# First batch of an attention-plus-experts kernel: one visit per head with split inputs, two sets of score banks, experts held back

## The chip, the cores and the metric

One core of one Trainium2 chip runs the whole program. The metric is the device time of one execution in microseconds (us), the median of three runs. Five instruction streams work side by side, each in its own fixed order: PE (TensorE, matmuls), DVE (VectorE), ACT (ScalarE), POOL (GpSimd) and SP (SyncE, which here only issues DMA transfers).

## The reference, cut to what matters

```python
batch, n_heads, seq, head_dim = (4, 8, 768, 64)
q_bucket, k_bucket = ...          # 6 sign bits of q @ proj and of k @ proj
mask   = q_bucket[:, :, :, None] == k_bucket[:, :, None, :]
scores = np.where(mask, 0.125 * q @ k.T, -1e9)
attn   = softmax(scores)          # per row; sum + 1e-9 below the line
x      = (attn @ v)  ->  [4 * 768 tokens, 8 * 64]
h      = x @ w_in                 # 512 -> 2048
g      = s * max(h, 0)**2 + b
out    = g @ w_out                # 2048 -> 512
```

All is float32. The first half is called attention below, the second half experts (the kernel's function is `moe`).

## The kernel before, in words

**Slots and visits.** Attention is cut into 96 slots: 4 batches x 8 heads x 3 chunks of 256 queries (`CH`). A visit is a stretch of slots of one head for which the head's inputs lie ready. In a slot, `scores` runs six leading matmuls (keys by queries, with the hash bits as extra rows) into three PSUM banks, DVE takes the maximum over keys (`mx`), PE transposes it, DVE reduces it again (`nmt`), PE transposes that, DVE builds a row of negated maxima (into `bq` or `zhl`), and six more matmuls ("rest") add that row to the banks. ACT takes the exponential of the three banks, and `values` multiplies by v. A reciprocal on DVE, `zpb`, comes once for two heads.

**Precision.** A float32 matmul takes several passes. A split input is a rounded part plus a remainder (`aq`/`bq` for queries, the two planes of `ks` for keys), so that matmuls on rounded operands can be used and the "rest" matmuls carry the remainders. Split inputs are made by `prep`: per head three `split` steps and three `hash_` steps, each PE, ACT and DVE, and then copies between buffers by SP's DMA queue, the last of them only after the third hash.

**The first batch before.** It is visited twice. In visits 0 to 7 (slots 0 to 7) each head's first chunk is computed with unsplit float32 inputs, kept in `EQ` and `EK`, which lie in the buffers that hold weights 16 to 31 later; the leading matmuls of these slots (L523) are full float32. In visits 8 to 15 (slots 8 to 23) the other two chunks of each head follow, from inputs that `resplit` derives from `EQ` and `EK`. Batches 1 to 3 (slots 24 to 95) are visited once, three slots to a visit. In the first batch the products with v are full float32 too (L582); later they use split exponentials, `hl`.

**Weights.** 32 tiles of w_in and w_out are decoded into split form while the first batch runs: a load on ACT's DMA queue, ACT L304 and L305, DVE L306 and L307, POOL L308, ACT L310 and POOL L316 each. `decodes` says how many are begun by slot i.

**Experts.** `moe(bb, c)` is one chunk of 256 tokens, over all eight heads: in 8 groups, 24 matmuls on w_in (L660) into bank 5 and 12 on w_out (L677) into banks 6 and 7. A chunk needs the last head's slot of that chunk number. There are 12 chunks, and `moe` steps have the lowest priority on PE, so they fill what attention leaves. They may start as soon as inputs and weights are there (`GATE = 0`).

**Banks.** Scores use banks 0 to 2 in every slot, so the leading matmuls of one slot wait for the exponentials of the slot before. Bank 3 takes the products with v, bank 4 the small transposes and `prep`.

**Order.** All steps go into `Plan`; `Plan.order` sets every engine's order in advance by a list scheduler with a cost per step, a cost `HOP` for passing a result to another engine, and `LOOK`, how far it will wait for a step of higher priority. On the chip each engine runs that order and waits on semaphores.

Of the kernel before, what the change touches and what calls it, by code (L numbers as in the profile page):

```python
# [22 lines left out]
EPS = 1e-9  # L23
# [8 lines left out]
class Plan:  # L32
# [25 lines left out]
    def order(self):  # L58
# [14 lines left out]
        while len(out) < n:  # L73
# [7 lines left out]
            i = min((i for i in open_[e] if ready[i] <= t + LOOK.get(e, 0.0)), key=lambda i: (self.steps[i][3], i))  # L81
# [22 lines left out]
HOP = {None: 0.0, PE: 0.2, DVE: 0.13, ACT: 0.2, POOL: 0.1, SP: 1.8}  # L104
SAME = {None: 0.0, PE: 0.2, DVE: 0.0, ACT: 0.05, POOL: 0.0, SP: 0.0}
LOOK = {PE: 0.0, DVE: 0.5, ACT: 0.2}
# [3 lines left out]
def lsh_attention_moe(ctx: ExitStack, tc, q, k, v, proj, w_in, w_out, s, b, out):  # L110
# [173 lines left out]
    def decode(u, pr):  # L284
# [19 lines left out]
        act(512, lambda: nc.scalar.activation(g, raw()[:, :, 1].bitcast(F32), AF.Copy, scale=float(2.0**-112)), rk + [("pace", u % PACE)], [gk], pr)  # L304
        act(512, lambda: nc.scalar.activation(raw()[:, :, 0], raw()[:, :, 0].bitcast(U32), AF.Copy, scale=float(2.0**-29)), rk, rk, pr)  # L305
        dve(256, lambda: nc.vector.tensor_scalar(raw()[:, :, 1], gi, -2**31, None, ALU.bitwise_and), [gk], rk, pr, 0.54)  # L306
        dve(512, lambda: nc.vector.scalar_tensor_tensor(gi, gi, 3, raw()[:, :, 1], ALU.logical_shift_left, ALU.bitwise_or), rk, [gk], pr, 0.88)  # L307
# [46 lines left out]
    def prep(w, i, pr):  # L354

        x, y, h, exact = visits[w]["x"], w % 2, visits[w]["h"], w < EARLY
        aq, bq, ks, nat = EQ[h] if exact else AQ[y], BQ[y], KS[y], NAT[y]
# [7 lines left out]
        def both(g, i, pr):  # L365

            pb = fill_bank()
            cols, o = slice(g * HS, (g + 1) * HS), bank[:, pb, 0:HS]

            def tr():  # L370
                for t in range(HT):
                    nc.tensor.transpose(out=bank[:, pb, t * P:(t + 1) * P], in_=nat[:, g * HT + t], identity=ident)
            pe(0.33, tr, NK, [("b", pb)], pr)
            act(HS, lambda: nc.scalar.activation(aq[:, cols], o, AF.Copy, scale=qk_sb), [("b", pb)], AK(x, g=thirds(g)), pr, 0.12)
            dve(HS, lambda: nc.vector.tensor_copy(EK[h][0:D, cols], o[D:P]), [("b", pb)], [("ks", x, g)], pr, 0.5)
            if g:
                ahead(pr)

        def split(g, i, pr):
            cols, o = slice(g * CH, (g + 1) * CH), bank[:, 4, CH:2 * CH]  # L380

            def tr():
                for t in range(TPC):
                    nc.tensor.transpose(out=bank[:, 4, CH + t * P:CH + (t + 1) * P], in_=nat[:, g * TPC + t], identity=ident)  # L384
            pe(0.23, tr, NK, [("b", 4, 1)], pr)
            act(CH, lambda: nc.scalar.activation(aq[:, cols], o, AF.Copy, scale=qk_sb), [("b", 4, 1)], AK(x, g=(g,)), pr, 0.12)
            dve(CH, lambda: nc.vector.scalar_tensor_tensor(bq[:, cols], o, qk_sb, f32(aq[:, cols]), ALU.mult, ALU.subtract), [("b", 4, 1)] + AK(x, g=(g,)), BK(x, g=(g,)), pr, 0.48)
# [408 lines left out]
```

## Time and profile before

| | us |
|---|---|
| median of 3 runs (lowest, highest) | 1117.24 (1116.52, 1120.74) |
| profiled execution, its own time | 1122.19 |
| its span from first to last instruction | 1120.4 |
| PE busy | 1061.0 |
| DVE busy | 657.1 |
| ACT busy | 702.5 |
| POOL busy | 683.9 |

A row of the timeline gives the start, the duration, the engine, the line, the operation, output and inputs, how often, and in brackets the idle time ahead of it and what ended it. A row of windows gives the stretch, its length, for each engine the busy time and in brackets the number of instructions, then the granted clock of PE as a share of full speed, the busy share of the DMA engines and the GB/s moved. A row of groups ends with busy time, mean duration in ns, idle time ahead and what ended that. `x6` in the timeline counts the profile's records; a full float32 matmul leaves two of them.

### The profile page before, as it was taken

How to read it: one execution, taken by the hardware profiler on the slowest of the kernel's cores; microseconds unless marked ns; L12 is line 12 of the kernel's file. 1: busy time of each engine (PE TensorE's matmuls, PEld its weight loads, DVE VectorE, ACT ScalarE, POOL GpSimd, SP SyncE). 2: the span in 40 equal slices, each digit the busy share in tenths (PEclk: the TensorE clock that was granted, in tenths of full speed). 3: DMA queues.
4: the chain of work that ended last, by engine and by line, in shares of the span. 5: the costliest groups of instructions: out<-in, count | busy, mean ns of one | idle time of the engine just before them, and what ended most of it. 6: DMA issues, size and time to landing. Idle time of an engine off the chain costs nothing.

```text
span 1120.4 us, 18819 instructions
## 1 busy us (share of the span) xinstructions
PE 1061.0 (95%) x6862; PEld 919.1 (82%) x6862; DVE 657.1 (59%) x807; ACT 702.5 (63%) x1377; POOL 683.9 (61%) x617
## 2 busy tenths in 40 slices
PE   8998788999999999989999999999999999999998
PEld 6665666878888888778888888888888998898987
DVE  6666576766767776766777676767776752000000
ACT  5556677766677667666767667677776765333332
POOL 5345898876777667656767676767676765222221
PEclk9888899999999999989999999999999999999999
DMA  8644454433322422332333242233233202101010
GB/s 173 160 138 129 131 138 113 131 96 86 89 73 69 133 61 73 90 88 56 78 100 91 53 130 61 76 81 98 63 81 86 70 1 85 39 19 57 1 57 19
DMA packets 99404, 94.49 MB, mean 84 GB/s; under 512 B 68528, under 2 KB 72112, under 8 KB 99312
## 3 DMA queue, kind: packets, MB, share of 16 engines
q1 hardware_dynamic: 94112, 76.24, 26.1%
q10 hardware_dynamic: 5200, 17.05, 5.0%
q8 instruction: 54, 0.88, 0.3%
q14 instruction: 38, 0.31, 0.1%
HBM read 49.81 MB, written 18.87 MB: 61 GB/s over the span
## 4 chain that ended last, share of the span: by engine, by line
PE 80%; DVE 7%; ACT 5%; DMA 3%; POOL 3%; issue 2%; SPq 0%; DVEq 0%; ACTq 0%; POOLq 0%
PE bank L660 23%; PE bank L677 21%; PE bank L555 5%; PE bank L525 5%; PE bank L582 4%; PE bank L585 4%; PE bank L584 4%; PE bank L523 2%; PE bank L534 2%; PE bank L384 2%; PE bank L612 2%; DVE mx L530 2%; DMA xd<-xsb 2%; DMA xc<-xd 1%; ACT et L560 1%
## 5 line engine op out<-in xcount | busy, mean ns | idle before, releaser
L578 POOL TENSOR_TENSOR hl<-et,hl 128x512 fp32r<-128x512 f32 x216 | 278.1, 1317 | 163.0 <-ACT hl L577 147.6
L660 PE MATMUL bank<-xc,w 128*128 128x256 f32 x2304 | 344.8, 288 | 9.5 <-DMA xc<-xd 8.0
L660 PEld LDWEIGHTS bank<-xc,w 128*128 128x128 f32 x2304 | 307.5, 191 | 20.9 <-DMA xc<-xd 9.3
L677 PE MATMUL bank<-w,ghb 128*128 128x512 f32 x768 | 256.3, 397 | 0.0
L668 POOL TENSOR_TENSOR glb<-rb,ghb 128x512 fp32r<-128x512 f32 x96 | 124.4, 1296 | 137.9 <-ACT ghb L667 130.0
L530 DVE TENSOR_REDUCE mx<-bank 128x256 f32<-128x1536 f32 x96 | 168.1, 1752 | 44.0 <-PE bank L525 25.7
L677 PE MATMUL bank<-w,glb 128*128 128x512 f32 x384 | 152.1, 400 | 0.5 <-POOL glb L668 0.5
L665 ACT ACTIVATE rb<-bank 128x512 f32<-128x512 f32 x96 | 57.1, 595 | 151.3 <-PE bank L660 148.7
L677 PEld LDWEIGHTS bank<-w,ghb 128*128 128x128 f32 x768 | 136.7, 189 | 17.2
L560 ACT ACTIVATE et<-bank 128x512 f32<-128x512 f32 x240 | 130.7, 624 | 31.2 <-PE bank L555 27.6
L606 DVE TENSOR_REDUCE zb<-et 128x256 f32<-128x1536 f32 x72 | 126.1, 1751 | 41.3 <-ACT et L560 41.0
L577 ACT CAST hl<-et 128x512 fp32r<-128x512 f32 x216 | 128.6, 661 | 0.8
L584 PE MATMUL bank<-hl,vs 128*128 128x256 f32 x432 | 121.6, 299 | 0.5 <-ACT hl L577 0.5
L525 PE MATMUL bank<-aq,ks 78*128 78x256 f32 x528 | 118.6, 308 | 1.4 <-ACT et L560 0.7
L585 PE MATMUL bank<-hl,vs 128*128 128x256 f32 x432 | 115.8, 288 | 2.9 <-POOL hl L578 2.5
L525 PEld LDWEIGHTS bank<-aq,ks 78*128 78x128 f32 x528 | 91.0, 194 | 12.6 <-ACT ex L560 2.0
L685 DVE SCALAR_TENSOR_TENSOR osb<-bank,misc,bcs 128x512 f32<-128x512 f32 x22 | 16.2, 744 | 132.4 <-PE bank L677 132.4
L585 PEld LDWEIGHTS bank<-hl,vs 128*128 128x128 f32 x432 | 82.5, 191 | 8.8 <-POOL hl L578 6.0
L555 PE MATMUL bank<-bq,ks 128*128 128x256 f32 x528 | 79.5, 287 | 9.6 <-DVE bq L544 8.3
L616 ACT ACTIVATE xpb<-bank,vmn 64x256 f32<-64x256 f32 x96 | 44.9, 468 | 69.3 <-PE bank L585 67.7
L584 PEld LDWEIGHTS bank<-hl,vs 128*128 128x128 f32 x432 | 82.1, 190 | 3.8 <-ACT hl L577 0.7
L622 DVE RECIPROCAL zpb<-zpb 128x256 f32<-128x256 f32 x48 | 83.7, 1743 | 2.3 <-ACT zpb L614 1.9
(111 smaller groups left out, 1662.9 us busy)
## 6 DMA issues: line engine op xcount, KB each, us to landing
xd<-xsb SPq DMA_DIRECT2D x48, 256.0 KB
xc<-xd SPq DMA_DIRECT2D x48, 256.0 KB
raw<-in_moe_w_in_dram ACTq DMA_DIRECT2D x16, 512.0 KB
raw<-in_moe_w_out_dram ACTq DMA_DIRECT2D x16, 512.0 KB
nat<-in_q_dram SPq DMA_DIRECT2D x32, 192.0 KB
nat<-in_k_dram SPq DMA_DIRECT2D x32, 192.0 KB
bq<-aq SPq DMA_DIRECT2D x32, 192.0 KB
out_dram<-osb SPq DMA_DIRECT2D x22, 256.0 KB
```

Source lines behind the costliest of these rows:

```text
L525: nc.tensor.matmul(o, ks[0:HR + TPC, 0, kt], aq[0:HR + TPC, cs], start=m == 0, stop=m == 1, skip_group_check=True)
L530: dve(S * TPC, lambda: nc.vector.tensor_reduce(t, sc, AX.XY, ALU.max), [("b", b) for b in pb], [tk], pr, 1.75)
L555: nc.tensor.matmul(o, ks[:, 1, kt], bq[:, cs], start=False, stop=m == 1, skip_group_check=True)
L560: act(512, lambda p=p, z=z: nc.scalar.activation(et(z) if plain(i) else pairs(z), bank[:, pb[p]] if plain(i) else bank[:, pb[p]].rearrange ...
L577: act(512, lambda z=z, y=y: nc.scalar.copy(HL[2 * y].rearrange("p (m n) -> p m n", n=CH), pairs(z)), [("e", z)], [("hl", 2 * y)], pr)
L578: pool(512, lambda z=z, y=y: nc.gpsimd.tensor_tensor(HL[2 * y + 1].rearrange("p (m n) -> p m n", n=CH), pairs(z), f32(HL[2 * y]).rearrange ...
L584: nc.tensor.matmul(av, VS[w % 2][:, kt], HL[2 * y][:, ms], start=(kt == 0), stop=False)
L585: nc.tensor.matmul(av, VS[w % 2][:, kt], HL[2 * y + 1][:, ms], start=False, stop=(kt == NT - 1))
L606: dve(S * TPC, lambda: nc.vector.tensor_reduce(ZB, es, AX.XY, ALU.add), [("e", z) for z in range(NE)], ["zb"], pr, 1.75)
L660: nc.tensor.matmul(hp, wt[("wi", n, cc)][:, m % 2, fs], xc[:, m // 2, :], start=(cc == 0 and m == 0), stop=(cc == NC_ - 1 and m == 2))
L668: pool(2 * CH, lambda r=r, gh=gh, gl=gl: nc.gpsimd.tensor_tensor(gl, r, f32(gh), ALU.subtract), [rk, hk], [lk], MP)
L677: nc.tensor.matmul(bank[:, 6 + t, :], (gh, gh, gl)[n][:, ts], wt[("wo", f)][:, n % 2], start=(f == 0 and n == 0), stop=(f == NF - 1 and n ...
```

## The change

- The first batch is visited like the others, once per head with three slots a visit; `EQ`, `EK`, `resplit`, the exact branches of `prep`, `scores` and `values`, and the code that tied decoding to the freed buffers are removed. All 32 weight tiles have their own buffers from the start.
- `ODD`: slots 1, 3, ..., 23 put their scores into banks 5 to 7, the experts' banks; even slots and all later ones use banks 0 to 2.
- `GATE = 23`: no step of the experts is put into the plan ahead of slot 23.
- `RATE = 1.3`: about 1.3 weight tiles per slot are begun in the first batch.
- `HOP`, `SAME`, `LOOK` and the costs of the two decoding steps on DVE have new values, and the choice of the next step in `order` has a new rule. They bear on the order of all slots.

```diff
@@ Plan.order @@
-            i = min((i for i in open_[e] if ready[i] <= t + LOOK.get(e, 0.0)), key=lambda i: (self.steps[i][3], i))
+            rank = lambda i: (self.steps[i][3], i)
+            i = min((i for i in open_[e] if ready[i] <= t), key=rank)
+            i = min((j for j in open_[e] if ready[j] <= t + LOOK.get(e, 0.0) * self.steps[i][1] and rank(j) <= rank(i)), key=rank)
...
-HOP = {None: 0.0, PE: 0.2, DVE: 0.13, ACT: 0.2, POOL: 0.1, SP: 1.8}
+HOP = {None: 0.0, PE: 0.2, DVE: 0.06, ACT: 0.06, POOL: 0.06, SP: 1.8}
...
-    for cs in ((0,), tuple(range(1, NCH))):
-        for h in range(H):
-            visit(0, h, cs)
-    for bb in range(1, B):
+    for bb in range(B):
         for h in range(H):
             visit(bb, h, tuple(range(NCH)))
...
-                    if exact:
-                        n = P if i < WARM else HR
-                        nc.tensor.matmul(o, EK[h][0:n, kt], EQ[h][0:n, cs], start=m == 0, stop=m == 1, skip_group_check=True)
-                        continue
                     nc.tensor.matmul(o, ks[0:HR + TPC, 0, kt], aq[0:HR + TPC, cs], start=m == 0, stop=m == 1, skip_group_check=True)
...
     def decodes(i):
...
+        return min(ND, int(FIRST + RATE * i))
...
-            parts = prep(w + 2, i, pr) if w + 2 in preps else resplit(w + 2, i, pr) if visits[w + 2]["x"] in (0, 1) else []
+            parts = prep(w + 2, i, pr)
...
-RATE = 1.0
-SPLIT = (0, 1, 2, 3, 4, 5, 6, 7)
+RATE = 1.3
 PACE = 2
-WARM = 3
-ODD = ()
-GATE = 0
+ODD = tuple(range(1, 24, 2))
+GATE = 23
```

The lines move: leading matmuls L523/L525 become L458, "rest" L553/L555 becomes L485, products with v L582 become L511, the maximum L530 becomes L463, `nmt` L536 becomes L469, the row of maxima L544 becomes L477, split L387 becomes L364, decode L306/L307 becomes L290/L291, the reciprocal L622 becomes L547, the experts' L660 and L677 become L585 and L602.

**PE in the first batch.** Before, at slots 13 and 14, the order on PE is: rest of the slot, then the next slot's leading matmuls in pairs, each behind the exponential that frees its bank, in turn with the products with v, and then the two small transposes of the next slot.

```order
L555 MATMUL bank<-bq_70,ks_72 128x256 x6
L525 MATMUL bank<-aq_69,ks_73 128x256 x2
L582 MATMUL bank<-ex_92,vs_994 128x256
L525 MATMUL bank<-aq_69,ks_73 128x256 x2
L582 MATMUL bank<-ex_92,vs_994 128x256
L525 MATMUL bank<-aq_69,ks_73 128x256 x2
L582 MATMUL bank<-ex_93,vs_994 128x256 x2
L582 MATMUL bank<-ex_94,vs_994 128x256 x2
L534 MATMUL bank<-ident,mx 128x128 x2
L538 MATMUL bank<-ident,nmt 2x128
```

Now, at slots 0 to 2, the leading matmuls of slot 2 (L458) stand ahead of the rest of slot 1 (the second L485), with slot 1's transposes of the maximum before and among them; those of slots 0 and 1 (twelve) stand together just above this piece.

```order
L471 MATMUL bank<-ident,nmt 2x128
L361 MATMUL bank<-ident,nat_66 128x128 x2
L485 MATMUL bank<-bq_70,ks_72 128x256 x6
L511 MATMUL bank<-et,vs_192 128x256 x4
L467 MATMUL bank<-ident,mx 128x128 x2
L511 MATMUL bank<-et,vs_192 128x256 x2
L458 MATMUL bank<-aq_68,ks_72 128x256 x2
L471 MATMUL bank<-ident,nmt 2x128
L458 MATMUL bank<-aq_68,ks_72 128x256 x4
L361 MATMUL bank<-ident,nat_66 128x128 x2
L485 MATMUL bank<-bq_70,ks_72 128x256 x6
```

What moved: the scores of a slot are computed while the slot before is still between its maximum and its exponentials.

**DVE in the first batch.** Before, in slots 13 to 15, one weight tile (L306, L307) stands between the row of maxima of one slot (L544) and the maximum of the next (L530), and no split steps.

```order
L530 TENSOR_REDUCE mx<-bank 128x256
L536 TENSOR_REDUCE nmt<-bank 128x2
L544 SCALAR_TENSOR_TENSOR bq_70<-bank,ident 2x256
L306 TENSOR_SCALAR raw_992<-osb 128x512
L307 SCALAR_TENSOR_TENSOR osb<-osb,raw_992 128x512
L530 TENSOR_REDUCE mx<-bank 128x256
L536 TENSOR_REDUCE nmt<-bank 128x2
L544 SCALAR_TENSOR_TENSOR bq_71<-bank,ident 2x256
L306 TENSOR_SCALAR raw_1042<-osb 128x512
L307 SCALAR_TENSOR_TENSOR osb<-osb,raw_1042 128x512
L530 TENSOR_REDUCE mx<-bank 128x256
```

Now, in slots 6 and 7, split steps (L364), decoding and the reciprocal (L547) stand inside the slots, between the three small steps.

```order
L463 TENSOR_REDUCE mx<-bank 128x256
L364 SCALAR_TENSOR_TENSOR bq_71<-bank,misc,aq_69 128x256
L469 TENSOR_REDUCE nmt<-bank 128x2
L290 TENSOR_SCALAR raw_201<-osb 128x512
L477 SCALAR_TENSOR_TENSOR bq_70<-bank,ident 2x256
L291 SCALAR_TENSOR_TENSOR osb<-osb,raw_201 128x512
L463 TENSOR_REDUCE mx<-bank 128x256
L547 RECIPROCAL zpb<-zpb 128x256
L469 TENSOR_REDUCE nmt<-bank 128x2
L290 TENSOR_SCALAR raw_202<-osb 128x512
L477 SCALAR_TENSOR_TENSOR bq_70<-bank,ident 2x256
L291 SCALAR_TENSOR_TENSOR osb<-osb,raw_202 128x512
```

What moved: three split and three hash steps per head came into these slots, and work stands in the places where DVE waits for PE's small transposes.

**The experts on PE.** Before, the first expert matmuls stand around the small transposes of slot 6, and from there on they fill PE in the first batch.

```order
L582 MATMUL bank<-ex_97,ek_88 65x256
L660 MATMUL bank<-xc_0_0_246,w_405 128x256 x2
L534 MATMUL bank<-ident,mx 128x128 x2
L384 MATMUL bank<-ident,nat_66 128x128 x2
L660 MATMUL bank<-xc_0_0_246,w_405 128x256
L660 MATMUL bank<-xc_0_0_246,w_419 128x256 x3
```

Now the first one stands behind the products with v of slot 23, and no expert matmul is ahead of it.

```order
L485 MATMUL bank<-bq_71,ks_73 128x256 x6
L361 MATMUL bank<-ident,nat_67 128x128 x2
L511 MATMUL bank<-ex_79,vs_194 128x256 x2
L511 MATMUL bank<-ex_80,vs_194 128x256 x2
L511 MATMUL bank<-ex_81,vs_194 128x256 x2
L585 MATMUL bank<-xc_0_0_226,w_362 128x256 x3
L585 MATMUL bank<-xc_0_0_226,w_396 128x256 x3
```

What moved: all expert work that PE did in the first batch stands behind it.

More of the change, by code (lines that the diff above doesn't have):

```diff
@@ L256, in visit @@
     def visit(bb, h, chunks):
-        visits.append({"bb": bb, "h": h, "x": len(visits) % 2 if bb or len(visits) >= H and h in SPLIT else f"e{h}"})
+        visits.append({"bb": bb, "h": h, "x": len(visits) % 2})
         for c in chunks:
             slots.append((bb, h, c, len(visits) - 1))
-    for cs in ((0,), tuple(range(1, NCH))):
-        for h in range(H):
-            visit(0, h, cs)
-    for bb in range(1, B):
+    for bb in range(B):
         for h in range(H):
@@ L268, in lsh_attention_moe @@
     NSL = len(slots)
-    EARLY = H
-    preps = [w for w, z in enumerate(visits) if z["bb"] or w < H]
+    preps = list(range(len(visits)))
     w_in_w = w_in.bitcast(I32)
@@ L363, in ahead, with half @@
                 load(preps[n], pr)
-        def both(g, i, pr):
+        def half():
+            if not wide:
+                return bank[:, 4, CH:2 * CH], [("b", 4, 1)]
             pb = fill_bank()
[L368 to L377, printed above, removed]
+            return bank[:, pb, 0:CH], [("b", pb)]
         def split(g, i, pr):
-            cols, o = slice(g * CH, (g + 1) * CH), bank[:, 4, CH:2 * CH]
+            cols = slice(g * CH, (g + 1) * CH)
+            o, ok = half()
             def tr():
                 for t in range(TPC):
[L384 to L387, printed above, removed]
+                    nc.tensor.transpose(out=o[:, t * P:(t + 1) * P], in_=nat[:, g * TPC + t], identity=ident)
+            pe(0.23, tr, NK, ok, pr)
+            act(CH, lambda: nc.scalar.activation(aq[:, cols], o, AF.Copy, scale=qk_sb), ok, AK(x, g=(g,)), pr, 0.12)
+            dve(CH, lambda: nc.vector.scalar_tensor_tensor(bq[:, cols], o, qk_sb, f32(aq[:, cols]), ALU.mult, ALU.subtract), ok + AK(x, g=(g,)), BK(x, g=(g,)), pr, 0.48)
             if g == NCH - 1:
@@ L489, in plain @@
     def plain(i):
-        return not slots[i][0] and (i < EARLY or slots[i][1] in PLAIN)
+        return not slots[i][0]
     def et(z):
@@ L581, in mm @@
                 if exact:
-                    nc.tensor.matmul(av[0:VW] if first else av, values_at(h, kt) if first else VS[w % 2][:, kt], et(z)[:, ms], start=(kt == 0), stop=(kt == NT - 1))
+                    nc.tensor.matmul(av, VS[w % 2][:, kt], et(z)[:, ms], start=(kt == 0), stop=(kt == NT - 1))
                     return
@@ L597, in values @@
         zs, zk = zz[r], [("b", 4, 0)]
[L598 to L602 removed]
+        if exact:
             zs, zk = av[D:P], [ak]
@@ L613, in values @@
             pe(mmc(CH, 2), total, ["zh", "zl"], [("b", 4, 0)], pr + 3)
-        act(CH, lambda: nc.scalar.activation(zpb[r, y], zs, AF.Copy, bias=0.0 if first else EPS), zk, [("zp", y, hh)], pr)
+        act(CH, lambda: nc.scalar.activation(zpb[r, y], zs, AF.Copy, bias=EPS), zk, [("zp", y, hh)], pr)
         n = bb % 2 * H + h
```

123 lines of the change are left out of this document (30 added, 93 removed).

## The prediction

> **What bounds the kernel now.** I read the page first (busy times), then the busy time of three stretches that I cut at the maxima of DVE, one per slot, and then the timeline at the cuts. First the page's busy line.
>
> ```profile
> PE 1061.0 (95%) x6862; PEld 919.1 (82%) x6862; DVE 657.1 (59%) x807; ACT 702.5 (63%) x1377; POOL 683.9 (61%) x617
> ```
>
> PE carries the time as a whole. The cuts are these maxima: of slots 0, 8, 13, 14, 24 and 95.
>
> ```profile
> 17.05 1.76 DVE L530 TENSOR_REDUCE mx<-bank 128x256 f32<-128x1536 f32 x1 [1.90 <-PE bank L523]
> ...
> 106.92 1.76 DVE L530 TENSOR_REDUCE mx<-bank 128x256 f32<-128x1536 f32 x1 [4.42 <-PE bank L525]
> ...
> 153.26 1.69 DVE L530 TENSOR_REDUCE mx<-bank 128x256 f32<-128x1536 f32 x1
> 159.95 1.76 DVE L530 TENSOR_REDUCE mx<-bank 128x256 f32<-128x1536 f32 x1 [1.47 <-PE bank L525]
> ...
> 244.30 1.76 DVE L530 TENSOR_REDUCE mx<-bank 128x256 f32<-128x1536 f32 x1 [0.29 <-PE bank L525]
> ...
> 920.22 1.76 DVE L530 TENSOR_REDUCE mx<-bank 128x256 f32<-128x1536 f32 x1
> ```
>
> The first batch takes until 244.3, the second pass of it (slots 8 to 24) at (244.30 - 106.92)/16 = 8.59 us a slot. Batches 1 to 3 run at (920.22 - 244.30)/71 = 9.52 us a slot. Busy times in the three stretches:
>
> ```profile
> 0.00:244.30 244.30, 214.41 (x1119) 162.42 (x1120) 162.12 (x225) 159.25 (x303) 161.63 (x138) 0.91 0.51 136
> 244.30:922.00 677.70, 652.67 (x4516) 582.28 (x4514) 478.93 (x563) 474.96 (x960) 467.73 (x434) 0.99 0.31 79
> 922.00:1120.40 198.40, 193.91 (x1232) 174.39 (x1230) 16.04 (x20) 68.28 (x115) 54.58 (x47) 1.00 0.12 39
> ```
>
> In the middle and last stretch PE is busy 652.67/677.70 and 193.91/198.40 of the time: there a matmul that is moved in costs its own time. In the first PE has 29.89 us of gaps and a clock of 0.91; DVE, ACT and POOL are each busy about two thirds. So the change trades a shorter first stretch against expert matmuls that it pushes into the last one.
>
> **Term 1, the experts' work that leaves the first batch.** The same first stretch for L660 alone, and then for L677 alone:
>
> ```profile
> 0.00:244.30 244.30, 25.79 (x142) 20.76 (x142) 0.91 0.51 136
> ...
> 0.00:244.30 244.30, 16.41 (x48) 8.31 (x48) 0.91 0.51 136
> ```
>
> 142 and 48 matmuls. Their price at the end, where nothing else is on PE, from a stretch of the tail:
>
> ```profile
> 954.52 3.04 PE L660 MATMUL bank<-xc,w 128*128 128x256 f32 x24
> 957.40 0.63 PE L677 MATMUL bank<-w,ghb 128*128 128x512 f32 x2
> ...
> 960.15 3.04 PE L660 MATMUL bank<-xc,w 128*128 128x256 f32 x24
> ```
>
> 24 of L660 take 957.40 - 954.52 = 2.88 us (0.12 each), 12 of L677 960.15 - 957.40 = 2.75 us (0.229 each). So 142 x 0.12 + 48 x 0.229 = +28.0 us, added behind the last slot. Nothing covers it, since the tail is PE alone.
>
> **Term 2, a hole that goes.** Between slots 48 and 50 PE ran dry: the experts of batch 0 were done, the inputs of batch 1 not yet loaded.
>
> ```profile
> 481.15 0.58 PE L660 MATMUL bank<-xc,w 128*128 128x256 f32 x1 [4.18 <-DMA xc<-xd]
> ...
> 472.52 1.75 DVE L530 TENSOR_REDUCE mx<-bank 128x256 f32<-128x1536 f32 x1
> 486.99 1.74 DVE L530 TENSOR_REDUCE mx<-bank 128x256 f32<-128x1536 f32 x1
> ```
>
> This slot took 14.47 us in place of 9.52. With experts begun only after slot 23, a further 28 us of their work is left at that place, so I take -5.0 us (bounds: -5.0 and 0, if another load is late in its place).
>
> **Term 3, the end of the first batch.** I write its new time as X = start + 24 p, against 244.3.
>
> Start: the first maximum came at 17.05. Now two heads go through split, hash and copies first. The nearest row for the copies is in batch 2, SP's four copies behind the third hash:
>
> ```profile
> 654.30 0.59 SPq L145 DMA_DIRECT2D aq<-bq  x1
> ...
> 656.86 0.75 SPq L145 DMA_DIRECT2D aq<-nat  x1
> ```
>
> Four take 3.3 us (one other issue among them); eight per head, 5.3 to 6.6. Against that the full float32 leading matmuls (below) go. Bounds 17 and 24; I take 20.
>
> The pace p: with two sets of score banks the chain of slot i+1 (leading matmuls) no longer waits for the exponentials of slot i. What is left is the engine with most work. DVE's groups:
>
> ```profile
> L530 DVE TENSOR_REDUCE mx<-bank 128x256 f32<-128x1536 f32 x96 | 168.1, 1752 | 44.0 <-PE bank L525 25.7 <-PE bank L523 12.0 <-ACT raw L305 3.5
> ...
> L622 DVE RECIPROCAL zpb<-zpb 128x256 f32<-128x256 f32 x48 | 83.7, 1743 | 2.3 <-ACT zpb L614 1.9
> L536 DVE TENSOR_REDUCE nmt<-bank 128x2 f32<-128x256 f32 x96 | 38.9, 405 | 48.6 <-PE bank L534 35.5 <-ACT rb L666 6.9 <-PE bank L384 4.8
> L414 DVE TENSOR_SCALAR nat<-bank,misc 44x256 f32<-44x256 f32 x72 | 38.2, 530 | 31.3 <-PE bank L411 28.2 <-ACT zpb L614 1.2 <-ACT hl L577 1.1
> L307 DVE SCALAR_TENSOR_TENSOR osb<-osb,raw 128x512 int32<-128x512 int32 x32 | 37.0, 1157 | 0.5
> L544 DVE SCALAR_TENSOR_TENSOR bq<-bank,ident 2x256 fp32r<-2x256 f32 x88 | 36.1, 410 | 58.4 <-PE bank L538 56.0 <-PE bank L384 1.4 <-ACT vmn L452 0.4
> L387 DVE SCALAR_TENSOR_TENSOR bq<-bank,misc,aq 128x256 fp32r<-128x256 f32 x72 | 34.3, 477 | 24.8 <-PE bank L612 17.1 <-PE bank L555 3.7 <-ACT aq L386 2.5
> ...
> L306 DVE TENSOR_SCALAR raw<-osb 128x512 int32<-128x512 int32 x32 | 21.7, 679 | 3.8 <-ACT osb L304 3.7
> ```
>
> Per slot: maximum 1.752, `nmt` 0.405, row 0.410, half a reciprocal 0.872, one split 0.477, one hash 0.530, and 32/24 weight tiles at 0.679 + 1.157, 2.448. Sum 6.89 us. ACT and POOL had 159.25 and 161.63 us in the old first stretch, at most 6.6 and 6.7 a slot; the conversions of `resplit` leave both and ACT gets one per split instead, so DVE stays above them. 6.89 is a floor: p there needs DVE never to wait. The other bound is the old 8.59, if the second bank set opens nothing. In the old first stretch DVE was busy 162.12/244.30 = 0.66, under a chain that held it; slot 13 to 14 took 6.69 us with one weight tile. In the new order decoding stands where DVE waits for PE's transposes, but a visit still begins with a wait: third hash, copies, then leading matmuls. I take DVE busy 0.87 of the time, p = 7.9, a little above the middle of 6.89 and 8.59. X = 20 + 24 x 7.9 = 209.6, that is -34.7 us.
>
> On the way PE loses the 96 records of full float32 leading matmuls (29.51 us busy in the old stretch, L523) and gets prep's split and hash matmuls for them; both lie inside X, as does the rest that moves: the 32 weight loads, 0.51 of the DMA engines' time over 244.3 us, would be 0.60 of 209.6, and SP issues eight copies per head in place of `resplit`'s six, 16 more at about 0.8 us over the whole stretch. The experts' new wait holds nothing up: in PE's order nothing stands behind it before slot 24, and their first inputs lie loaded.
>
> ```profile
> 0.00:244.30 244.30, 29.51 (x96) 22.07 (x96) 0.91 0.51 136
> ```
>
> **Term 4, the order of the other 72 slots.** Same steps, other scheduler numbers. PE's gaps there are 677.70 - 652.67 = 25.0 us, 5 of which are term 2. A better order can take back at most the other 20, a worse one may add as much; I take 0 and keep 10 us either way for the range.
>
> **The sum** against the profiled execution: 28.0 - 5.0 - 34.7 + 0 = -11.7; span 1120.4 to 1108.7. That execution took 1122.19, 1.8 more than its span and 4.95 more than the median 1117.24. So 1108.7 + 1.8 - 4.95 = 1105.6, and I say 1106 us. No change lies at X = 244.3 - 23.0 = 221.3, p = 8.39. Half a per cent, about what a measurement of this kernel can tell from no change, is 5.6 us, or 0.23 us of p: below 8.15 the kernel is faster, above 8.62 slower.
>
> **The rivals.**
>
> *The clock (slower).* Without experts PE has gaps in the first batch, and its clock may fall to half. Stretches of 4 us in the old second pass:
>
> ```profile
> 116.00:120.00 4.00, 1.42 (x7) 0.59 (x5) 4.00 (x5) 3.48 (x7) 4.00 (x5) 0.92 0.12 20
> 120.00:124.00 4.00, 3.63 (x13) 3.33 (x14) 2.56 (x4) 3.15 (x7) 3.48 (x4) 0.50 0.22 42
> ...
> 156.00:160.00 4.00, 3.22 (x19) 2.70 (x20) 1.99 (x4) 3.41 (x7) 4.00 (x3) 1.00 0.28 32
> 160.00:164.00 4.00, 2.68 (x14) 1.75 (x13) 3.02 (x4) 2.52 (x5) 3.92 (x5) 1.00 0.84 271
> ```
>
> Ahead of the second row lies one wait of PE, on `nmt`:
>
> ```profile
> 118.87 0.27 PE L538 MATMUL bank<-ident,nmt 128*2 128x128 f32 x1 [1.44 <-DVE nmt L536]
> ```
>
> After 1.42 busy of 4 the clock was 0.50; after 3.22 and 2.68 it stayed at 1.00. A slot's own work on PE, in the undisturbed slot 14:
>
> ```profile
> 156.74 0.98 PE L555 MATMUL bank<-bq,ks 128*128 128x256 f32 x6 [0.50 <-DVE bq L544]
> 157.99 0.51 PE L525 MATMUL bank<-aq,ks 78*128 78x256 f32 x2 [0.28 <-ACT ex L560]
> ...
> 159.68 1.89 PE L582 MATMUL bank<-ex,vs 128*128 128x256 f32 x8
> 161.76 0.44 PE L534 MATMUL bank<-ident,mx 128*128 128x128 f32 x2 [0.19 <-DVE mx L530]
> 162.72 0.27 PE L538 MATMUL bank<-ident,nmt 128*2 128x128 f32 x1 [0.52 <-DVE nmt L536]
> ```
>
> 0.98 + 3.58 (157.99 to 159.68 + 1.89) + 0.44 + 0.27 = 5.3 us, and split and hash on top, about 0.6 for two transposes and three hash matmuls at the 0.12 that one of L660 takes: 5.9 at full clock. In 7.9 us that is 3.0 of every 4, on the side that stayed fast. At a mean clock c PE alone needs 5.9/c: above p = 8.62, and so slower, once c is under 0.68. At c = 0.65, p = 9.1, X = 238, the time is 1106 + 28 = 1134. I give this 0.17. The Trainium skill ("TensorE: Matmul & The Clock Gate", HAM oscillation) says that only PE-idle gaps over about 3 us bring the clock back to half. By that rule the new stretch, whose gaps are shorter, would keep its clock and this rival would fall away, with the sum as it stands. The trace does not agree with it here: the gap before 118.87 was 1.44 us, and the clock halved.
>
> *The chain stays (no change).* DVE's order is still maximum, `nmt`, row, next maximum; if waits at visit starts and late copies keep p between 8.15 and 8.62, gain and moved expert work cancel: 1112 to 1123 us, say 1117. For it: a visit's copies start only after its third hash, and in the best 28 us of the first batch DVE was busy 22.00, 0.79:
>
> ```profile
> 140.00:168.00 28.00, 23.66 (x137) 19.33 (x135) 22.00 (x22) 20.49 (x39) 25.40 (x21) 1.00 0.52 138
> ```
> Against: slot 13 to 14 at 6.69 us with the one bank set. 0.20.
>
> *The order pays (faster still).* If half of the 20 us of PE gaps in batches 1 to 3 go as well: 1096. For it: PE's L534 at 161.76 started 0.05 us after its maximum ended (159.95 + 1.76), where the old table reckons 0.13; against: PE is busy 0.96 there already. 0.11.
>
> **How the numbers follow.** My forecast 0.52, the order on top 0.11, chain 0.20, clock 0.17. Faster 0.63, same 0.20, slower 0.17. The forecast's own range is p from 7.3 to 8.15, 1091 to 1112. The range leaves out about 0.2 (0.06 below, 0.14 above): 1088 (p = 7.3 and a few us from the order) to 1125 (the chain's case whole, and the mild end of the clock's).
>
> **What would show it.** The maximum of slot 24 near 210 and the first at 20; DVE busy near 0.87 and PE's clock above 0.85 up to there; no expert matmul before it; no PE wait of 4 us for the experts' inputs near the end of batch 1; the tail behind the last maximum near 198 + 28 - 5 = 221 us. Wrong if slot 24 comes after 221, if the 72 later slots run at another pace than 9.5 with more gaps on PE, or if the tail grows by more than 28.

## The result, and the profile after

The change made the kernel slower: 1177.34 us (median of 4 runs, 1176.6 to 1178.19) against 1116.92 us (median of 4 runs on the same chip), a ratio of 1.0536 (95% interval 1.0514 to 1.0558). The forecast was 1106 us, range 1088 to 1125. The profiled execution has a span of 1175.9 us, 55.5 more than that of before. Executions that fell into a slower state of the chip (one of e8 below, 1651.66 us at a clock of 0.55; with it e8's median would be 1146.33) are left out of the times and ratios.

The busy line of the page after:

```profile
PE 1063.2 (90%) x6838; PEld 928.9 (79%) x6838; DVE 644.5 (55%) x807; ACT 680.5 (58%) x1353; POOL 648.3 (55%) x592
```

PE is busy 2.2 us longer than before (1061.0), so 53.3 of the 55.5 us are time in which it waits. The cuts are again DVE's maxima (L463 now), of slots 0, 8, 9, 24 and 95:

```profile
32.35 1.76 DVE L463 TENSOR_REDUCE mx<-bank 128x256 f32<-128x1536 f32 x1 [17.52 <-PE bank L458]
...
92.23 1.73 DVE L463 TENSOR_REDUCE mx<-bank 128x256 f32<-128x1536 f32 x1
...
108.59 1.76 DVE L463 TENSOR_REDUCE mx<-bank 128x256 f32<-128x1536 f32 x1 [5.74 <-PE bank L458]
...
262.18 1.76 DVE L463 TENSOR_REDUCE mx<-bank 128x256 f32<-128x1536 f32 x1 [7.01 <-PE bank L458]
...
940.18 1.76 DVE L463 TENSOR_REDUCE mx<-bank 128x256 f32<-128x1536 f32 x1
```

The windows between them (stretch, length, busy time of PE, PEld, DVE, ACT, POOL, granted clock, DMA share, GB/s):

```profile
0.00:32.35 32.35, 12.60 (x82) 11.25 (x83) 8.84 (x33) 6.48 (x13) 1.42 (x8) 0.71 0.67 154
32.35:262.18 229.83, 171.45 (x840) 133.92 (x839) 133.96 (x186) 121.18 (x246) 111.41 (x94) 0.81 0.46 126
262.18:940.18 678.00, 648.08 (x4457) 575.72 (x4456) 482.38 (x566) 471.52 (x959) 471.40 (x437) 0.98 0.31 79
940.18:1175.90 235.72, 231.06 (x1464) 208.03 (x1462) 19.29 (x23) 81.30 (x136) 64.08 (x54) 1.00 0.10 35
```

Against before, slot 24 comes 17.9 us later (262.18, not 244.30), the next 71 slots take 2.1 more (678.00, not 675.92), and the tail 35.5 more (235.72, not 200.18): 55.5 together. In the first batch the clock is 0.81 and DVE busy 133.96/229.83 = 0.58.

What makes the tail, from windows of the experts' two lines: after, L585 and then L602, in the first, middle and last stretch; the same of before, L660 and then L677, in the middle and the last.

```profile
0.00:262.18 262.18, 1.42 (x9) 1.22 (x9) 0.80 0.49 129
262.18:940.18 678.00, 212.07 (x1359) 184.74 (x1359) 0.98 0.31 79
940.18:1175.90 235.72, 121.51 (x936) 119.11 (x936) 1.00 0.10 35
...
262.18:940.18 678.00, 201.59 (x662) 114.50 (x663) 0.98 0.31 79
940.18:1175.90 235.72, 122.00 (x491) 87.99 (x489) 1.00 0.10 35
```

```profile
244.30:920.22 675.92, 215.81 (x1370) 186.06 (x1370) 0.99 0.31 79
920.22:1120.40 200.18, 103.24 (x792) 100.71 (x792) 1.00 0.12 39
...
244.30:920.22 675.92, 207.56 (x696) 118.58 (x696) 0.99 0.31 79
920.22:1120.40 200.18, 101.44 (x410) 73.52 (x408) 1.00 0.12 39
```

144 more matmuls of the first kind and 81 of the second stand behind the last slot: 144 x 0.12 + 81 x 0.229 = 35.8 us, the whole of the 35.5. The first batch gave up 133 and 48 of them (27.0 us); the middle, which was to take more, did 11 and 34 fewer (9.1 us). (A record at a window's border counts on both sides, so 48 and 34 make 82.)

What makes the first batch: one visit's start, slot 8 to slot 9, from the timeline. Rows are the three split steps of the head that slot 9 needs (PE L361, at 67.73, 77.34, 87.76), its third hash on DVE (97.67), its copies on SP's queue, the leading matmuls and the maximum.

```profile
67.73 0.44 PE L361 MATMUL bank<-ident,nat 128*128 128x128 f32 x2 [0.52 <-DVE bq L477]
...
77.34 0.63 PE L361 MATMUL bank<-ident,nat 128*128 128x128 f32 x2
...
87.76 0.63 PE L361 MATMUL bank<-ident,nat 128*128 128x128 f32 x2
89.36 1.93 SPq L147 DMA_DIRECT2D ks<-aq  x3
...
97.67 0.54 DVE L381 TENSOR_SCALAR nat<-bank,misc 44x256 f32<-44x256 f32 x1 [0.66 <-PE bank L378]
...
99.78 0.60 SPq L147 DMA_DIRECT2D aq<-bq  x1
...
103.03 0.77 SPq L147 DMA_DIRECT2D aq<-nat  x1
...
106.94 2.47 PE L458 MATMUL bank<-aq,ks 78*128 78x256 f32 x10 [5.30 <-DMA aq<-nat]
```

The head's buffers come free only when the visit before last ends, and from there the preparation is one chain: splits 10 us apart, a first round of copies with the hashes beside it, a second round that may overwrite `aq` only when the first has landed, and its landing. From the third hash's end (98.21) to the first leading matmul 8.7 us pass; for the last 5.3 of them PE stands idle, its work on the slots at hand done. The chains of two heads also hold each other up: in PE's fixed order the second split of this head stands behind the leading matmuls of the visit before, which themselves waited for copies:

```profile
75.47 2.08 PE L458 MATMUL bank<-aq,ks 78*128 78x256 f32 x8 [3.39 <-DMA aq<-nat]
```

Within visits 2 to 7 the maxima stand 7.6 us apart on the mean; across the starts of visits 3 to 7 and of slot 24 15.6 us. The waits in 0 to 262 us, of SP's queue (us in total, times, longest):

```profile
SPq L147 <- DMA ks<-aq: 47.4, 11, 6.9
```

The second round of copies stands behind the landing of the first. What PE waited for ahead of its leading matmuls, from 52 to 262 us (with one more of 4.0 us, put down to v's load, 31.6 us together):

```profile
PE bank L458 <- DMA aq<-nat: 20.3, 4, 6.3
PE bank L458 <- DMA xd<-xsb: 7.3, 1, 7.3
```

### The profile page after: what moved, and what is told of

Same layout as the page of the kernel before. It is cut to its first block, busy times and chain, and to the rows that moved or that the text cites. A ratio compares the mean times of both kernels' runs of the same rounds, so it can differ in the third digit from the quotient of the medians.

```text
span 1175.9 us, 18700 instructions
## 1 busy us (share of the span) xinstructions
PE 1063.2 (90%) x6838; PEld 928.9 (79%) x6838; DVE 644.5 (55%) x807; ACT 680.5 (58%) x1353; POOL 648.3 (55%) x592
## 4 chain that ended last, share of the span: by engine, by line
PE 65%; DVE 3%; DMA 3%; ACT 3%; POOL 2%; issue 2%; SPq 1%; DVEq 0%; ACTq 0%; POOLq 0%
PE bank L585 21%; PE bank L602 20%; PE bank L485 4%; PE bank L458 4%; PE bank L514 4%; PE bank L513 3%; DMA xc<-xd 2%; PE bank L467 2%; PE bank L537 2%; PE bank L361 1%; POOL hl L507 1%; PE bank L376 1%; ACT aq L363 1%; PE bank L471 1%; DVE nmt L469 1%
## 5 line engine op out<-in xcount | busy, mean ns | idle before, releaser
L585 PE MATMUL bank<-xc,w 128*128 128x256 f32 x2304 | 335.0, 286 | 8.7 <-DMA xc<-xd 7.3
L585 PEld LDWEIGHTS bank<-xc,w 128*128 128x128 f32 x2304 | 305.1, 190 | 18.8 <-DMA xc<-xd 4.7
L602 PE MATMUL bank<-w,ghb 128*128 128x512 f32 x768 | 257.3, 396 | 0.4 <-ACT ghb L592 0.4
L463 DVE TENSOR_REDUCE mx<-bank 128x256 f32<-128x1536 f32 x96 | 168.0, 1750 | 63.9 <-PE bank L458 58.9
L458 PE MATMUL bank<-aq,ks 78*128 78x256 f32 x576 | 124.4, 319 | 51.3 <-DMA aq<-nat 38.4
L602 PE MATMUL bank<-w,glb 128*128 128x512 f32 x384 | 153.6, 401 | 0.6 <-POOL glb L593 0.6
L602 PEld LDWEIGHTS bank<-w,ghb 128*128 128x128 f32 x768 | 137.8, 188 | 18.2 <-ACT ghb L592 0.6
L458 PEld LDWEIGHTS bank<-aq,ks 78*128 78x128 f32 x576 | 99.0, 213 | 61.9 <-issue 24.5
L490 ACT ACTIVATE et<-bank 128x512 f32<-128x512 f32 x240 | 130.5, 622 | 29.4 <-PE bank L485 25.1
L485 PE MATMUL bank<-bq,ks 128*128 128x256 f32 x576 | 94.6, 303 | 6.9 <-DVE bq L477 6.7
L363 ACT ACTIVATE aq<-bank,misc 128x256 fp32r<-128x256 f32 x96 | 45.3, 475 | 96.0 <-PE bank L361 38.0
L292 POOL TENSOR_TENSOR osb<-osb,raw 128x512 int32<-128x512 int32 x32 | 42.1, 1318 | 90.4 <-DVE osb L291 54.5
L485 PEld LDWEIGHTS bank<-bq,ks 128*128 128x128 f32 x576 | 80.8, 202 | 14.2 <-DVE bq L477 13.1
```

The costliest lines, as they stand in the source:

```text
L458: nc.tensor.matmul(o, ks[0:HR + TPC, 0, kt], aq[0:HR + TPC, cs], start=m == 0, stop=m == 1, skip_group_check=True)
L463: dve(S * TPC, lambda: nc.vector.tensor_reduce(t, sc, AX.XY, ALU.max), [("b", b) for b in pb], [tk], pr, 1.75)
L485: nc.tensor.matmul(o, ks[:, 1, kt], bq[:, cs], start=False, stop=m == 1, skip_group_check=True)
L490: act(512, lambda p=p, z=z: nc.scalar.activation(et(z) if plain(i) else pairs(z), bank[:, pb[p]] if plain(i) else bank[:, pb[p]].rearrange ...
L585: nc.tensor.matmul(hp, wt[("wi", n, cc)][:, m % 2, fs], xc[:, m // 2, :], start=(cc == 0 and m == 0), stop=(cc == NC_ - 1 and m == 2))
L602: nc.tensor.matmul(bank[:, 6 + t, :], (gh, gh, gl)[n][:, ts], wt[("wo", f)][:, n % 2], start=(f == 0 and n == 0), stop=(f == NF - 1 and n ...
```

## The experiments

Theories: A, a visit's start waits for the serial preparation of its head; B, the new scheduler numbers make the order worse; C, decoding and weight loads beside it stretch that preparation; D, the second bank set costs something; and the clock. "Slot 24" is the start of its maximum: 262.18 after, 244.30 before. "A visit" is the mean distance between the first maxima of visits 2 to 7 and slot 24: 30.8 us after (the expectation of e5 counts visit 1 in); before, three slots took 26.2 over the same slots. "Within" and "across" are the mean distances of maxima as above, 7.6 and 15.6 us after. e3 to e7, e9, e12 and e13 were run once each.

**e1_oldsched**, the changed kernel with the old numbers, also for `SAME`, `LOOK`, the rule of choice and DVE's decoding costs:

```diff
-HOP = {None: 0.0, PE: 0.2, DVE: 0.06, ACT: 0.06, POOL: 0.06, SP: 1.8}
+HOP = {None: 0.0, PE: 0.2, DVE: 0.13, ACT: 0.2, POOL: 0.1, SP: 1.8}
```

> The changed kernel with the scheduler's old numbers and rule (HOP, SAME, LOOK, decoding costs). Theory A (between two visits of the first batch PE waits for the next head's split inputs: six small steps through half a bank, then two rounds of copies): the first batch keeps its pace, slot 24 at 255 to 275 us, 1165 to 1190 us. Rival B (the new numbers order the first batch badly): slot 24 at 215 or sooner, at most 1130 us.

Measured: 1162.56 us, ratio 1.0391 (1.0360 to 1.0421); slot 24 at 249.18, tail 235.5. Both lie a few us under the ranges of A and far above those of B. The numbers cost some 15 us of the 60, 13.0 of them in the first batch; the tail doesn't move. As the only cause, B falls.

**e2_newsched_on_before**, the new numbers on the kernel before.

> The kernel before with the new scheduler numbers and rule alone. Theory A: 1107 to 1127 us, the numbers move it by under 1%. Rival B (the numbers cost the time): 1150 us or more.

Measured: 1121.22 us, ratio 1.0032 (1.0000 to 1.0064), no change that can be told. The numbers hurt only in the new order.

**e3_decode_late**, all decoding and weight loads behind the first batch:

```diff
-        return min(ND, int(FIRST + RATE * i))
+        return 0 if i < 23 else min(ND, int(FIRST + RATE * (i - 23)))
```

> The changed kernel with all decoding of weights put after slot 23, so no weight loads and no decoding work in the first batch; only the first batch is to be read, the experts come later. Theory A (serial steps and copies): the visits still take about 27 us or more each, slot 24 at 235 us or later. Rival C (the weight loads on the DMA engines and decoding in the queues of DVE, ACT and POOL stretch the steps and the copies): visits of 18 to 21 us, first maximum near 20, slot 24 at 165 to 195 us.

Measured: slot 24 at 207.59, a visit 22.6 us, first maximum at 28.45 (1265.79 us in all, since the experts wait for weights).

```profile
207.59 1.76 DVE L463 TENSOR_REDUCE mx<-bank 128x256 f32<-128x1536 f32 x1 [1.04 <-PE bank L458]
```

This lies between the two ranges. The decoding, which was to lie in the engines' gaps, and its loads cost 54.6 us of the first batch here, the largest effect of one edit. C has a large share; a visit of 22.6 us without it is still 7.5 a slot, where visit 0, with its inputs ready, takes 6.0 in the changed kernel (32.35 to 50.28 for three).

**e4_one_bank_set**, `ODD = ()` and `GATE = 0`.

> The changed kernel with scores in banks 0 to 2 in all slots and no gate for the experts (whose first inputs need slot 21 in any case). Theory A (the wait lies between visits, not in the banks): visits of 30 to 35 us, slot 24 at 260 to 290 us, 1175 to 1205 us. Rival D (the second set of banks and the gate cost the time): slot 24 at 230 or sooner, at most 1150 us.

Measured: 1171.07 us (4 under the range of A), slot 24 at 261.74. D falls, and `GATE` bears on nothing: the first expert chunk needs the last head's slot 21, so hardly any expert work was there to be held back. In the order before, that slot was number 7. The second bank set does work inside a visit, 7.6 us within in place of 9.4 here, but the visit's start takes it back (15.6 across, not 11.0).

**e5_loads_only**, the loads at their old pace, called with their slot as `at`, the decoding steps behind slot 23:

```diff
+        if at is not None:
+            plan.add(ACT, 0.1, lambda: nc.scalar.dma_start(raw(), src.rearrange("p (n t) -> p n t", t=2)), KK(0) if u < PACE else [("nm", at % 4)], rk, pr - 5, 5.0)
+            return
```

> The changed kernel with the 32 weight loads left at their old pace through the first batch, but every decoding step (ACT, DVE, POOL) only after slot 23. With neither (the run before, all of it late) the maximum of slot 24 stood at 207.6 and a visit took 23.2 us on the mean of visits 2 to 8, against 262.2 and about 30 with both. If it is the transfers that slow the copies of the next head, visits stay at 27 us and more and slot 24 comes at 240 to 265. If it is the decoding steps in the engines' queues, the loads cost little: visits of 22 to 25 us, slot 24 at 200 to 222. The whole time says nothing here (about 1260, since the experts come late).

Measured: slot 24 at 223.23, a visit 25.1 us: 1.2 and 0.1 us past what the decoding steps were to give. Of the 54.6 us of e3, the loads alone bring 15.6, and the decoding steps on top of them 39.0.

**e6_wide**, `wide = w < H` in place of `w < 2`, and `ODD = ()`: split and hash through three banks.

> The changed kernel with the one score bank set (as in the run without the second set, 1171.1 us, slot 24 at 261.7) and with split and hash of every head of the first batch through the three free banks in place of one half bank, so that three splits, and then three hashes, no longer wait for each other's bank. If the serial steps through the half bank are most of the 30 us that a head's preparation takes: visits of 22 to 26 us, slot 24 at 215 to 240, time 1130 to 1155. If the copies, or the buffer set that comes free late, decide: slot 24 at 250 to 268, time 1160 to 1180.

Measured: 1173.6 us, slot 24 at 271.67, 4 us above the second range, a visit 30.4. Without the shared half bank a visit is no shorter, but the wait changes place: across it is 8.1 us, within 11.1, and from 52 to 271 us PE now waits for the load of the next head's v, whose column sums (L414) come next in its order:

```profile
PE bank L414 <- DMA vs<-in_v_dram: 26.4, 6, 7.0
```

So the half bank alone doesn't set the length of a visit; what does in e6, beyond that wait, no run isolates.

**e7_no_round1**, without the first round of copies in visits 2 to 7:

```diff
+        copy = (lambda *x: None) if 2 <= w < H else dma
...
-                dma(lambda: ks[0:D, 0], lambda: aq[D:P], AK(x, r=(1,)), KK(x, (0,)), pr, D * S * 4)
+                copy(lambda: ks[0:D, 0], lambda: aq[D:P], AK(x, r=(1,)), KK(x, (0,)), pr, D * S * 4)
...
```

> The changed kernel without the four copies behind the third split (k rows and the low half of k into the key tile) for visits 2 to 7; their keys are then those of an earlier head. If the eight copies carry the wait at a visit's start: the second round no longer waits behind the first, visits of 20 to 25 us, slot 24 at 205 to 230. If the first round lies beside the hash steps: visits of 27 us and more, slot 24 at 245 to 262.

Measured: 1155.76 us; slot 24 at 241.11 lies between the two ranges, a visit of 28.1 us in the second. The first round costs about 21 us in all.

**e8_three_sets**, a third set of head buffers in the weight buffers 27 to 31; `after_(w)` is w + 3 in the first batch:

```diff
+    third = [wk.tile([P, 1024], F32R, tag=f"w{u}", name=f"set{u}") for u in range(28, 32)]
...
+    def bset(w):
+        return w % 3 if w < H else w % 2
...
-            parts = prep(w + 2, i, pr)
+            parts = prep(after_(w), i, pr)
```

> The changed kernel with a third set of head buffers for visits 0 to 7, laid into the weight buffers 27 to 31 until those weights are loaded (after visit 5), so that a head may be prepared while the two ahead of it are visited; all the work stays. If the wait for the buffer set, and so the serial preparation behind it, sets the pace: visits begin with their inputs ready, 6 to 7.5 us a slot, slot 24 at 180 to 215, time 1095 to 1130. If the amount of work beside it, the decoding steps or the halved clock, sets the pace: slot 24 at 240 and more, time 1150 to 1180.

Measured: 1144.08 us, ratio 1.0210 (1.0141 to 1.0278). Slots 0, 24 and 95:

```profile
34.97 1.76 DVE L478 TENSOR_REDUCE mx<-bank 128x256 f32<-128x1536 f32 x1 [14.09 <-PE bank L473]
...
226.68 1.76 DVE L478 TENSOR_REDUCE mx<-bank 128x256 f32<-128x1536 f32 x1 [3.94 <-PE bank L473]
...
899.63 1.76 DVE L478 TENSOR_REDUCE mx<-bank 128x256 f32<-128x1536 f32 x1
```

35.5 us of the first batch go with the wait for a buffer set, with nearly all the decoding in place (28 tiles are begun on DVE ahead of slot 24, 30 in the changed kernel). From 52 to 227 us PE's waits ahead of leading matmuls for transfers shrink from 31.6 us to this one:

```profile
PE bank L473 <- DMA aq<-nat: 3.1, 1, 3.1
```

So A is shown as a cause. It and C shorten the same chain, so the 35.5 us here and the 54.6 of e3 don't add up. Maxima now stand 8.8 us apart across a visit's start and 8.5 within a visit. The pace is (226.68 - 34.97)/24 = 7.99: visits 0 and 1 took 5.7 and 6.6 us a slot, visits 2 to 7 8.6. The forecast of 6 to 7.5 was missed, and slot 24 lies between the two ranges; what sets the 8.6, with the inputs ready, no run isolates. The tail is 1146.8 - 899.63 = 247.2 us, 47 over that of before, so the kernel stays slower.

**e10_three_old**, three sets with the old numbers.

> Three sets of head buffers (slot 24 at 226.7, 1146.3 us) with the old scheduler's numbers, rule and decoding costs, which took 13.0 us off the maximum of slot 24 of the changed kernel with two sets. If the two add: slot 24 at 212 to 218, time 1128 to 1136, still slower than the kernel before, since the tail behind the last maximum stays at 235 to 247 against 200. If the old numbers only made up for waits at the visits' starts that three sets take away: slot 24 at 222 to 230, time 1140 to 1150.

Measured: 1136.04 us, ratio 1.0167 (1.0106 to 1.0229), slot 24 at 229.77. Slot 24 fits the second reading, the time is 4 us under it. The first batch is no shorter than in e8, as it would be if in e1 the old numbers had made up for waits that three sets remove. The 10 us between the profiled executions of the two lie behind slot 24 (907 us from there to the end, not 920). It is the fastest one-visit kernel here, and still slower than before.

**e12_prep_first**, preparation ranked first in the order (`pr - 20`).

> The changed kernel with the preparation steps of the first batch's heads ranked ahead of the running slot's own steps (20 points earlier in the order), two buffer sets as before. In the changed kernel the three splits of a head start about 10 us apart. If they stand late in the engines' orders, behind decoding and the running slots: splits 2 to 5 us apart, slot 24 at 225 to 245, time 1140 to 1160. If they wait for the buffer set and for the slots they stand between anyway: slot 24 at 252 to 268, time 1167 to 1182.

Measured: 1180.99 us, slot 24 at 254.42, a visit 29.2. The second split of the head for slot 9 came at 71.08, not 77.34, but the third still at 86.44 (87.76 in the changed kernel): rank does not bring that one forward. It waits until ACT has read (L394) v's column sums out of the half bank that both use:

```profile
86.44 0.69 PE L361 MATMUL bank<-ident,nat 128*128 128x128 f32 x2 [0.70 <-ACT vmn L394]
```

As in e4 and e6, the wait across a visit's start shrank (10.3 us) and the slots within grew (9.5). In all three runs a visit stays near 30 us: the length of the preparation shows in the whole visit, not only in the wait at its start.

**The clock: e9_warm, e11_three_old_warm, e13_dense_filler.** Matmuls of no use, wherever PE's order had nothing else.

> The changed kernel with small matmuls of no use (ones times ones, 128 columns, 12 steps of 4 a slot up to slot 20) that PE runs into the spare half bank wherever the order has nothing else for it; all the work stays. It keeps PE occupied at the visits' starts, where the granted clock fell to about 0.78. If the halved clock makes the slow pace: clock of the first batch above 0.92, the leading matmuls at a visit's start at 1 us in place of 2.9, slot 24 at 215 to 240, time 1130 to 1155. If the clock only follows the waits for the next head's inputs: clock up, but slot 24 still at 252 to 268, time 1165 to 1182.

> The same with three sets and old numbers, and with the small matmuls of no use beside it (10 steps of 4 a slot). With the visits' inputs ready the chain within a slot is left, in which PE's steps run at a clock of 0.86. If the clock matters there: slot 24 8 to 20 us earlier than without them, time 1112 to 1126. If the useless matmuls get in the way of the chain, or the clock costs nothing beside DVE and ACT: slot 24 within 4 us of the run without them, or later.

> The changed kernel with useless matmuls of 256 columns (the shape of the experts' first matmuls, 0.12 us each at full clock), 5 steps of 4 a slot up to slot 20, wherever PE's order has nothing else. Steps are reckoned with their true length this time. If such matmuls keep the clock and the halved clock is a cause: clock above 0.92 in the first batch, slot 24 at 225 to 248. If the clock rises and slot 24 stays at 252 or later, the clock only follows. If the clock stays near 0.80, this too tells nothing about cause, but says that PE busy alone does not bring the clock back.

Measured: 1318.44, 1224.76 and 1223.35 us, slot 24 at 421.89, 327.10 and 328.05. The clock of the first batch was 0.72, 0.91 and 0.82. None of the three says anything on the cause: the fillers went through the half bank that the preparation uses and changed the order of all engines, and in the first two a step of four took 0.46 us at full clock and 0.87 at half, with 0.26 planned. They say something on the clock itself (last section).

**e14_fill_the_wait**, the same order on every engine, fillers (`FILL = 36`) only where PE waits for copies:

```diff
+            fill = FILL if not p and not c and 2 <= w < H else 0
+                for _ in range(fill):
+                    nc.tensor.matmul(bank[:, pb[0], 0:CH], oner, zhl[:, 0], start=True, stop=True)
```

> The changed kernel, same order on every engine, with 36 useless matmuls of 256 columns (4.3 us at full clock) into the bank that the leading matmuls are about to fill, ahead of the first leading matmul of visits 2 to 7. They stand where PE waits 5 to 17 us for the copies of the new head. If the clock that halves over this wait is a cause of its own: the twelve leading matmuls at a visit's start take about 1.6 us in place of 2.9, the clock of the first batch rises from 0.80 to 0.88 or more, and each visit gains 2 to 5 us: slot 24 at 232 to 250, time 1145 to 1165. If it only follows: slot 24 at 255 to 275, time 1170 to 1190. If the wait after the fillers is still long enough to halve it: clock below 0.84, and cause stays open.

Measured: 1178.83 us, ratio 1.0539 (1.0495 to 1.0583), slot 24 at 264.61. The windows of the first batch, and two visits' starts (L460 fillers, L463 leading matmuls):

```profile
31.48:264.61 233.13, 190.90 (x1056) 155.06 (x1055) 133.70 (x185) 121.43 (x246) 111.97 (x94) 0.86 0.46 124
```

```profile
102.03 4.58 PE L460 MATMUL bank<-zhl,oner 128*128 128x256 f32 x36
107.94 1.67 PE L463 MATMUL bank<-aq,ks 78*128 78x256 f32 x12 [1.34 <-DMA bq<-aq]
...
230.34 2.90 PE L463 MATMUL bank<-aq,ks 78*128 78x256 f32 x12 [3.57 <-DMA xd<-xsb]
```

In four of the six visits the leading matmuls ran at full clock (1.6 to 1.7 us for twelve where they stood together, not 2.9), and those four took 127.4 us together, against 130.7 in the changed kernel: 0.8 us each, not 2 to 5. The other two took 60.0 against 54.2. At a visit's start the halved clock follows the wait; it is not what makes the visit long. The mean clock reached 0.86, so for the stretches within visits that isn't shown.

## Why the prediction was wrong, step by step

**Term 3, the start (20, measured 32.35: +12.4 us).** The copies were priced at SP's issue times, 3.3 us for four. What counts is their landing: in the changed kernel's start the first round was issued at 8.07, the copies of the second that overwrite `aq` could begin only at 17.88, the last of them went out at 23.16 and the first leading matmul ran at 30.66. With loads and decoding put off (e3) the first maximum comes at 28.45, with only the first two loads beside it (e5) at 28.75. So up to 3.9 us go to the decoding and the loads that follow (the next two go out at 22.49); which of them, no run separates.

```profile
8.07 2.02 SPq L147 DMA_DIRECT2D ks<-aq  x3
...
17.88 0.62 SPq L147 DMA_DIRECT2D aq<-bq  x1
...
23.16 0.77 SPq L147 DMA_DIRECT2D aq<-nat  x1
...
30.66 1.65 PE L458 MATMUL bank<-aq,ks 78*128 78x256 f32 x6 [17.27 <-DMA aq<-nat]
```

**Term 3, the pace (7.9, measured 9.58: +40.2 us).** This is the step that failed. The prediction saw that "a visit still begins with a wait: third hash, copies, then leading matmuls", and gave it a place inside 7.9 us a slot. The old 8.59 was taken as the upper bound, but it came from visits whose inputs `resplit` derived from `EQ` and `EK`, with no split and hash steps. The chain that does the whole preparation stood in the old batches 1 to 3, covered by a visit of 3 x 9.52 = 28.6 us, and it was never held against 3 x 7.9 = 23.7 us. Within a visit the maxima stand 7.6 us apart, less than 7.9; the 15.6 across its start were missed. e8 takes that wait away and gives 7.99, but that it meets 7.9 is luck: the mean comes from two quick visits and six at 8.6 us a slot, and DVE was busy 131.31/191.73 = 0.68 there and 0.58 in the changed kernel, not 0.87. So DVE's floor did not set the pace in either.

**Terms 1 and 2 (+23, measured +35.5).** Term 1 was right in size (28.0; 27.0 left the first batch). Term 2 had the wrong sign: the middle was to take up 5 us of expert work and did 9.1 less. Nearly all of that lies in the 28 us after slot 24. There the clock was 0.74 and L602 ran 4 times, against 36 of L677 in the kernel before, where the first chunk had long begun (L585 ran 39 times, L660 50). The windows of L602, then of L677:

```profile
262.18:290.18 28.00, 1.35 (x4) 0.68 (x4) 0.74 0.39 102
```

```profile
244.30:272.30 28.00, 10.79 (x36) 6.21 (x36) 1.00 0.39 110
```

A hole stayed too, now between slots 54 and 55, 14.2 us long, with one wait of 3.3 us for the experts' inputs. Even with X at 209.6 the sum would have been -34.7 + 2.1 + 35.5 = +2.9, no gain.

**Term 4** (0, bounds 10) measured +2.1, though PE did 9.1 us less of the experts' work there: it was busy 648.08 of 678.00 us, before 651.12 of 675.92, so its gaps grew from 24.8 to 29.9.

**The rivals.** *The chain stays* named the mechanism and bounded it too low (p up to 8.62). *The clock* named, at the visits' starts, a symptom: it fell to 0.81 where over 0.85 was forecast, not under the 0.68 at which that rival decides, and in e14 lifting it at four visits' starts brought 0.8 us each; its part within visits stays open. *The order pays* fell: in the new order the numbers cost 15 us (e1).

The prediction also set the row at 118.87, a wait of 1.44 us, against the Trainium skill ("TensorE: Matmul & The Clock Gate", HAM oscillation). That reading left out the waits around the row. The windows of 1 us around it, of the kernel before, and the next row of PE:

```profile
117.00:118.00 1.00, 0.41 (x2) 0.19 (x2) 1.00 (x1) 1.00 (x3) 1.00 (x2) 1.00 0.23 37
118.00:119.00 1.00, 0.13 (x1) 0.08 (x1) 1.00 (x3) 0.99 (x3) 1.00 (x2) 1.00 0.03 6
119.00:120.00 1.00, 0.14 (x1) 0.00 (x0) 1.00 (x2) 0.54 (x2) 1.00 (x2) 0.67 0.00 0
...
120.37 1.65 PE L555 MATMUL bank<-bq,ks 128*128 128x256 f32 x6 [1.23 <-DVE bq L544]
```

PE was busy 0.68 of these 3 us: small transposes split a long, nearly idle stretch into waits of 1.44 and 1.23 us, and the row at 118.87 alone can't be called the cause. No single wait here reaches the gap of some 3.4 us that the Trainium skill states in that section, so read by single waits this trace does not agree with it. e14 agrees nearly: after waits of 3.57 us (and 3.12 at another start) the clock was halved, after 1.34 us it was not.

## What to carry to other kernels

Before a step of preparation is moved into a shorter visit, add up its whole chain, from the moment its buffers come free to the landing of its last transfer, and hold that sum against the time until the inputs are needed; a row that shows the chain "covered" only shows the pace that covered it. A transfer's price on a chain is issue to landing, and a second transfer that overwrites what the first reads waits for that landing (here from 8.07 to 17.88 us). Work moved into gaps is free only if no chain runs through the same queues: the decoding steps, harmless by busy time (DVE 0.58), cost 39 us here (e5 against the changed kernel).

## What the runs showed of the hardware

PE busy does not by itself bring the clock back; which matmuls keep it busy matters. In e9 72 matmuls of 128 columns stood back to back at a visit's start for 15.6 us, 0.217 us each, and the clock stayed at 0.50 throughout. Two more such stretches, of 16.5 and 18.2 us (at 248.80 and 302.35), stayed at 0.50 as well.

```profile
93.24 15.62 PE L625 MATMUL bank<-oner 128*128 128x128 f32 x72 [0.63 <-DVE nat L381]
```

```profile
94.00:98.00 4.00, 4.00 (x21) 4.00 (x20) 1.73 (x3) 1.25 (x2) 2.63 (x2) 0.50 0.76 205
```

The same matmuls hold a clock that is already full. Later in e9, 84 of them ran for 9.6 us, 0.114 us each, at a clock of 1.00 (about what a matmul of 256 columns takes, 0.12):

```profile
200.19 9.59 PE L625 MATMUL bank<-oner 128*128 128x128 f32 x84 [0.20 <-DVE nat L381]
```

```profile
204.00:208.00 4.00, 4.00 (x38) 4.00 (x38) 1.37 (x1) 0.00 (x0) 0.82 (x1) 1.00 0.29 108
```

Matmuls of 256 columns did bring it back. In e13 forty of them began at 281.48 with the clock just halved, and within the fourth us it was full again:

```profile
281.48 6.42 PE L626 MATMUL bank<-zhl,oner 128*128 128x256 f32 x40 [0.63 <-DVE nat L382]
```

```profile
283.00:284.00 1.00, 1.00 (x7) 1.00 (x7) 0.00 (x0) 0.00 (x0) 0.00 (x0) 0.50 0.78 215
285.00:286.00 1.00, 1.00 (x11) 1.00 (x10) 0.00 (x0) 0.00 (x0) 0.00 (x0) 1.00 0.13 52
```

So in these runs the narrow matmuls kept a full clock, and in no stretch of over 3 us of them was a halved one restored. Why is not settled.
